# Layer 2 of a mixed FNet/H3 kernel: two sums of the Fourier matrix made by accumulating transfers instead of VectorE

## The chip, the core and the metric

The kernel runs on one core of a Trainium2 chip. A core has TensorE (PE, matrix products, with its weight loads listed apart as PEld), VectorE (DVE), ScalarE (ACT), GpSimd (POOL) and SyncE (SP), which here only issues transfers. Transfers are carried by 16 DMA engines and can be issued from SP, ACT and POOL. The metric is the device time of one execution in microseconds.

## The reference

Four layers follow one another on a stream `x` of 2048 x 576 float32. The first and the third are the FNet mixing, the second and the fourth an H3 block:

```python
def _A_ref(x, Cr, Ci, Wr, Wi):
    a = jnp.einsum("bsd,ed->bse", x, Wr)
    b = jnp.einsum("bsd,ed->bse", x, Wi)
    return jnp.einsum("ts,bse->bte", Cr, a) - jnp.einsum("ts,bse->bte", Ci, b)
...
x = x + _A_ref(_layernorm(x), ...)
x = x + _B_ref(_layernorm(x), ...)   # short conv, times v, long conv by FFT, gate q
x = x + _A_ref(_layernorm(x), ...)
x = x + _B_ref(_layernorm(x), ...)
```

`Cr` and `Ci` are 2048 x 2048 matrices given as inputs. The result is a real part, `Cr a - Ci b`. The change is in the second FNet layer, called layer 2 in the kernel.

## The kernel before, in words

The kernel multiplies with the sequence matrices first and with the hidden matrices afterwards. All products are float32 made of rounded halves: `split` (L90 to L92) rounds a tile to float32r with an ACT copy (L91, the high half) and takes the rest with a DVE subtraction (L92, the low half). A product then is three matmuls: high by high, high by low, low by high, all of them issued through `mm` at L74.

The order in time is: layer 0 (four blocks of 512 output rows) with the convolution branch woven into it; the first block of layer 2, made directly, up to about 803 us; blocks 1, 2 and 3 of layer 2, made by the Strassen scheme in `strassen()`; and at last the hidden products of layer 2 with the gating and the output, from about 1076 us on.

Strassen treats the real and the imaginary matrix and the two halves of the sequence as a 2 x 2 block matrix. A block `tb` has seven products in the order 5, 1, 6, 2, 7, 3, 4 (`ORDER`), each of four steps `kp`, so 28 steps for a block. A step multiplies two column tiles of C (`i` = 0 and 1, together 128 x 1024 words or 512 KB), and each column tile takes 6 matmuls into two PSUM banks, and 2 more for the remaining columns in products 5, 1, 2 and 4. In the text, "block 1, product 7, step 0" is the first step of the product 7 in `tb` = 1, and the three blocks start at about 803.3, 894.0 and 984.6 us.

`load_step` gets the C operand of a step into SBUF, unsplit:

- product 5: the imaginary matrix, first half plus second half. Two loads of 512 KB, one into a `csum` buffer and one into a `cw` buffer, and a DVE addition of 128 x 1024 words (L881). The sum stays in `SUM[kp]`.
- products 1 and 2: one load into `cw`, which is the operand, and a DVE addition of it onto `SUM[kp]` (L891).
- products 6 and 3: `SUM[kp]` as it then stands.
- product 7: the real plus the imaginary matrix, first half. Two loads into two `cw` buffers and a DVE addition (L887).
- product 4: one load into `cw`.

There are four `cw` buffers, three in the region `ph` and one in the region `flts`, and four `csum` buffers, all in `flts`; so a row of the profile that reads `flts,ph` in one of these additions has its `csum` or one `cw` buffer in `flts`. Buffers are used in turn, and the next load into a buffer waits for the last reader of what it held. The loads go out on SP (`load_after`, L161), in one order, and SP waits in order.

`ahead` keeps the load calls four steps and the split calls five column tiles in front of the matmuls. Five `cs` buffers hold the split column tiles, so the split of a column tile can't begin before TensorE has finished with the fifth one before it. Each engine runs its own instructions in order and waits at each for what it reads. In block 3, SP also brings back weights (`mats<-wd`) and results of earlier blocks (`ud`) between these loads.

POOL issues transfers for the convolution branch (L165) and computes powers for the norms (L177, L631). It has neither between the start of block 1 and 1076 us.

Of the kernel before, what the change touches and what calls it, by code (L numbers as in the profile page):

```python
# [13 lines left out]
OP = mybir.AluOpType  # L14
# [4 lines left out]
J = S // P  # L19
# [45 lines left out]
def fnet_h3_kernel(ctx: ExitStack, tc: tile.TileContext, x, c_mat, w_re, w_im, k_pad, v, shift_k,  # L65
                   ssm_k, ssm_d, f1c, i2c, midc, out):
    nc = tc.nc
# [91 lines left out]
    def load_after(dst, src):  # L159
        with tc.issue_after(anchor[-1]):  # L160
            return nc.sync.dma_start(dst, src).ins  # L161
# [689 lines left out]
    def post(tag="post"):  # L851
        return two(ring[tag]())
# [17 lines left out]
    def raw_c(g, tb, s2, kp, tag="cw"):  # L870
        t = post(tag)
        k = 2 * kp + (J // 2 if s2 else 0)
        anchor.append(load_after(t, c_mat[g, tb, k:k + 2].rearrange("k p n -> p k n")))
        return t

    SUM, RAW, HU = {}, {}, {}

    def load_step(tb, m, kp):
        if m == 5:
            src = SUM[kp] = raw_c(1, tb, False, kp, "csum")  # L880
            nc.vector.tensor_tensor(src, src, raw_c(1, tb, True, kp), OP.add)  # L881
        elif m in (6, 3):
            src = SUM[kp]
        elif m == 7:
            r = raw_c(1, tb, False, kp)
            src = raw_c(0, tb, False, kp)
            nc.vector.tensor_tensor(src, src, r, OP.add)  # L887
        else:
            src = raw_c(1 if m == 4 else 0, tb, m != 1, kp)
            if m in (1, 2):  # L890
                nc.vector.tensor_tensor(SUM[kp], SUM[kp], src, OP.add)  # L891
        RAW[tb, m, kp] = src
# [29 lines left out]
    def ahead(loads, halves):  # L922
        while len(RAW) < min(loads, len(steps)):
            load_step(*steps[len(RAW)])
        while len(done) < min(halves, 2 * len(steps)):
            h = len(done)
            done.append(h)
            cs[h] = split_half(steps[h // 2], h % 2)
# [197 lines left out]
```

## Time and profile before

| | us |
|---|---|
| median of 3 runs | 1201.41 |
| lowest, highest | 1200.62, 1201.98 |
| span of the profiled execution | 1198.9 |
| TensorE busy in the span | 1178.8 |
| VectorE busy | 839.6 |
| ScalarE busy | 665.4 |
| GpSimd busy | 74.7 |

The span runs from the first to the last instruction of one execution; the page gives no other time for that execution. The median of the runs lies 2.5 us above the span. The DMA share over the span is 53.9% for the queue of SP, 10.2% for that of ACT and 3.9% for that of POOL. In the profile a busy TensorE is modelled from pipelined matmuls, so its waits are best read from the idle time before an instruction and from the chain of waits.

### The profile page before, as it was taken

What the parts mean: (1) busy time and instruction counts of PE and PEld (TensorE: products, weight loads), DVE (VectorE), ACT (ScalarE), POOL (GpSimd) and SP (SyncE); (2) the same over time, 40 slices, a digit from 0 to 9 for tenths busy, and PEclk for the clock granted to TensorE, in tenths of its full rate; (3) what the DMA queues carried; (4) which work ended last, traced back from release to release, by engine and by line L of the source; (5) the groups of instructions that cost most, each with busy time, mean ns of one, the idle gap of its engine ahead of it and who ended that gap; (6) DMA issues with size and microseconds to landing.
All of it is one profiled execution on the core that took longest, in us unless ns stands there. A gap on an engine that the chain in (4) does not pass through costs nothing.

```text
span 1198.9 us, 18258 instructions
## 1 busy us (share of the span) xinstructions
PE 1178.8 (98%) x6320; PEld 1025.6 (86%) x6320; DVE 839.6 (70%) x1498; ACT 665.4 (55%) x1335; POOL 74.7 (6%) x116
## 2 busy tenths in 40 slices
PE   7999999999999999999999999999999999999997
PEld 6888888988888888888988898888888888789997
DVE  7899983679777677675347766775776777774764
ACT  7855665679877668774435666544444445450210
POOL 2210000000000000001101121000000000001111
PEclk9999999999999999999999999999999999999999
DMA  9869898546766667648967686872682677795621
GB/s 356 292 225 311 282 299 243 188 133 184 219 188 199 213 172 210 193 134 267 291 207 233 221 255 212 272 267 71 216 283 72 208 285 260 238 338 156 218 88 40
DMA packets 146110, 261.95 MB, mean 218 GB/s; under 512 B 15841, under 2 KB 44769, under 8 KB 146018
## 3 DMA queue, kind: packets, MB, share of 16 engines
q1 hardware_dynamic: 102674, 205.58, 53.9%
q10 hardware_dynamic: 36432, 42.63, 10.2%
q0 software_dynamic: 6912, 12.59, 3.9%
q8 instruction: 49, 0.80, 0.3%
q14 instruction: 43, 0.35, 0.1%
HBM read 194.09 MB, written 66.65 MB: 217 GB/s over the span
## 4 chain that ended last, share of the span: by engine, by line
PE 89%; ACT 4%; DVE 3%; DMA 2%; issue 2%; POOL 0%; ACTq 0%; SPq 0%; POOLq 0%; DVEq 0%
PE s L74 50%; PE bk L74 34%; PE rm L74 5%; ACT flts L490 2%; ACT mid L490 1%; DMA flts<-in_c_mat 1%; DVE mats L92 0%; ACT mats L91 0%; ACT u L91 0%; DMA flts<-in_ssm_k 0%; DMA ph<-in_c_mat 0%; DMA wd<-w 0%; DVE u L92 0%; DVE mid L496 0%; DVE f1f L386 0%
## 5 line engine op out<-in xcount | busy, mean ns | idle before, releaser
L74 PE MATMUL s<-mats 128*128 128x512 f32 x2088 | 535.0, 391 | 1.2 <-DVE u L92 0.5
L74 PEld LDWEIGHTS s<-mats 128*128 128x128 f32 x2088 | 380.0, 188 | 70.1 <-DVE u L92 1.1
L92 DVE TENSOR_TENSOR mats<-flts,mats 128x512 fp32r<-128x512 f32 x206 | 140.9, 688 | 63.8 <-ACT mats L91 63.3
L91 ACT ACTIVATE mats<-flts 128x512 fp32r<-128x512 f32 x206 | 128.5, 628 | 84.5 <-PE bk L74 32.3
L74 PEld LDWEIGHTS bk<-mid 128*128 128x128 f32 x768 | 116.2, 188 | 21.7 <-ACT flts L490 8.1
L74 PE MATMUL bk<-mid 128*128 128x288 f32 x768 | 132.5, 299 | 2.2 <-ACT flts L490 2.0
L74 PE MATMUL bk<-w,u 128*128 128x288 f32 x864 | 120.9, 296 | 0.3 <-ACT flts L490 0.3
L74 PEld LDWEIGHTS bk<-w,u 128*128 128x128 f32 x864 | 117.4, 188 | 4.0 <-ACT flts L490 1.9
L496 DVE TENSOR_TENSOR mid<-flts,mid 128x576 fp32r<-128x576 f32 (+1 forms) x149 | 93.5, 628 | 35.2 <-ACT mid L490 32.7
L490 ACT ACTIVATE flts<-bk 128x288 f32<-128x288 f32 x160 | 62.2, 405 | 90.1 <-PE bk L74 81.0
L74 PE MATMUL rm<-mats 128*128 128x512 f32 x304 | 94.9, 391 | 0.0
L490 ACT ACTIVATE flts<-flts 64x288 f32<-64x288 f32 x192 | 85.0, 443 | 5.5
L490 ACT ACTIVATE mid<-flts 128x576 fp32r<-128x576 f32 (+1 forms) x148 | 80.3, 575 | 6.0 <-DMA flts<-t 3.0
L436 ACT ACTIVATE flts<-bk 128x288 f32<-128x288 f32 x128 | 49.3, 410 | 49.9 <-PE bk L74 41.3
L74 PE MATMUL bk<-f1r 128*128 128x288 f32 x384 | 64.2, 300 | 7.7 <-ACT f1r L91 7.6
L74 PEld LDWEIGHTS bk<-f1r 128*128 128x128 f32 x384 | 59.0, 191 | 14.8 <-ACT f1r L91 8.6
L280 DVE TENSOR_TENSOR flts<-flts,bk 128x288 f32<-128x288 f32 x48 | 21.8, 453 | 67.6 <-PE bk L74 67.6
L74 PE MATMUL bk<-mats 128*128 128x288 f32 (+1 forms) x376 | 67.8, 317 | 0.0
L74 PEld LDWEIGHTS rm<-mats 128*128 128x128 f32 x304 | 56.9, 188 | 12.3 <-DVE flts L266 0.3
L74 PE MATMUL s<-t,mats 128*128 128x512 f32 x264 | 64.9, 389 | 0.0
L177 POOL TENSOR_TENSOR flts<-flts 128x1 f32<-128x1 f32 x35 | 29.4, 841 | 522.2 <-DVE flts L176 522.2
L74 PE MATMUL bk<-mats,t 128*128 128x288 f32 (+1 forms) x368 | 59.3, 303 | 0.0
(145 smaller groups left out, 1505.4 us busy)
## 6 DMA issues: line engine op xcount, KB each, us to landing
flts<-in_c_mat SPq DMA_DIRECT2D x148, 256.0 KB, 3.8
ph<-in_c_mat SPq DMA_DIRECT2D x54, 512.0 KB, 4.5
t<-flts ACTq DMA_DIRECT2D x64, 288.0 KB, 4.5
flts<-in_c_mat SPq DMA_DIRECT2D x30, 512.0 KB, 5.3
flts<-t SPq DMA_DIRECT2D x53, 288.0 KB, 2.9
vd<-flts ACTq DMA_DIRECT2D x64, 144.0 KB, 2.3
flts<-vd SPq DMA_DIRECT2D x32, 288.0 KB, 4.5
mid<-in_i2c POOLq DMA_DIRECT2D x32, 256.0 KB, 4.9
```

Source lines behind the costliest of these rows:

```text
L74: nc.tensor.matmul(ps, lhsT, rhs, start=first, stop=last, skip_group_check=more)
L91: a = nc.scalar.activation(h, src, AF.Copy).ins
L92: return a, nc.vector.tensor_tensor(l, src, h.bitcast(F32), OP.subtract).ins
L177: pows.append(nc.gpsimd.tensor_tensor(rs, ve, mhalf, OP.pow).ins)
L280: added[:] = [nc.vector.tensor_tensor(r[:, cs], r[:, cs], ps[:, :HD], OP.add).ins]
L436: stored[:] = [nc.scalar.activation(so[:, c, :], ps[:, :HD], AF.Copy).ins]
L490: last_act.append(nc.scalar.activation(*args, **kw).ins)
L496: nc.vector.tensor_tensor(l, src, h.bitcast(F32), OP.subtract)
```

## The change

In products 5 and 7 of a block, the second of the two matrices is no longer loaded into a buffer of its own and added by VectorE. The first one is loaded by SP as before, into the `csum` buffer (product 5) or a `cw` buffer (product 7), and then a transfer issued from GpSimd reads the second one from memory and adds it onto that buffer (`accum_op=OP.add`). That makes 24 additions and 24 loads from SP fewer, and 24 transfers from GpSimd more. In product 7 the operands change places: the imaginary matrix is loaded, and the real one is added. A `cw` buffer is no longer taken for the second matrix.

```diff
+    def add_c(t, g, tb, s2, kp):
+        k = 2 * kp + (J // 2 if s2 else 0)
+        nc.gpsimd.dma_start(t, c_mat[g, tb, k:k + 2].rearrange("k p n -> p k n"), accum_op=OP.add)
+
     SUM, RAW, HU = {}, {}, {}

     def load_step(tb, m, kp):
         if m == 5:
             src = SUM[kp] = raw_c(1, tb, False, kp, "csum")
-            nc.vector.tensor_tensor(src, src, raw_c(1, tb, True, kp), OP.add)
+            add_c(src, 1, tb, True, kp)
         elif m in (6, 3):
             src = SUM[kp]
         elif m == 7:
-            r = raw_c(1, tb, False, kp)
-            src = raw_c(0, tb, False, kp)
-            nc.vector.tensor_tensor(src, src, r, OP.add)
+            src = raw_c(1, tb, False, kp)
+            add_c(src, 0, tb, False, kp)
         else:
             src = raw_c(1 if m == 4 else 0, tb, m != 1, kp)
```

The order of the matmuls is the same in both kernels, and the other instructions of VectorE and ScalarE keep their order but for a few splits and stores.

## The prediction

> **What bounds the kernel.** I read the page's busy rows first, then the stages of layer 2 as time windows, TensorE's waits, and the chain that ended last.
>
> ```profile
> span 1198.9 us, 18258 instructions
> PE 1178.8 (98%) x6320; PEld 1025.6 (86%) x6320; DVE 839.6 (70%) x1498; ACT 665.4 (55%) x1335; POOL 74.7 (6%) x116
> ```
>
> TensorE is the bound over the whole span. The windows of the Strassen blocks say whether that holds where the edit is:
>
> ```profile
> core 0: us, PE busy (x) PEld busy (x) DVE busy (x) ACT busy (x) POOL busy (x), PEclk, DMA share, GB/s
> 832.30:857.70 25.40, 25.40 (x114) 21.04 (x113) 19.07 (x25) 11.22 (x19) 0.00 (x0) 1.00 0.43 131
> 894.00:984.60 90.60, 90.60 (x400) 74.83 (x399) 62.93 (x84) 39.24 (x64) 0.00 (x0) 1.00 0.59 189
> 1039.00:1050.00 11.00, 10.07 (x45) 8.02 (x44) 6.96 (x10) 5.16 (x10) 0.00 (x0) 1.00 0.88 256
> ```
>
> Block 2 (894.0 to 984.6) has 400 matmuls without a gap, with VectorE at 62.93 of 90.60 us and POOL at nothing. Only the window from 1039 is short of TensorE work, by 0.93 us. TensorE's waits from 803 to 1077 us are one line, and the chain of waits shows what lies behind it:
>
> ```profile
> PE s L74 <- DVE mats L92: 0.9, 1, 0.9
> ```
>
> ```profile
> 1040.01 5.14 DMA flts<-in_c_mat
> ...
> 1045.24 1.23 DVE flts L887
> 1046.47 0.61 DVE mats L92
> ...
> 1047.12 12.99 PE s L74 x56
> ```
>
> This is product 7 of block 3. The last of its additions (L887) stood on VectorE waiting for a transfer until 1045.24; the low half of a column tile that was long in SBUF came behind it, and TensorE waited for that one. So all that VectorE's additions cost the end of the program is 0.9 us.
>
> **What the change removes.** 24 additions:
>
> ```profile
> L881 DVE TENSOR_TENSOR flts<-flts,ph 128x1024 f32<-128x1024 f32 x9 | 11.0, 1222 | 10.5 <-DMA ph<-in_c_mat 10.5
> L887 DVE TENSOR_TENSOR flts<-flts,ph 128x1024 f32<-128x1024 f32 x6 | 7.3, 1225 | 10.0 <-DMA flts<-in_c_mat 9.9
> L887 DVE TENSOR_TENSOR ph<-ph 128x1024 f32<-128x1024 f32 x6 | 7.3, 1220 | 1.3 <-DMA ph<-in_c_mat 1.3
> L881 DVE TENSOR_TENSOR flts<-flts 128x1024 f32<-128x1024 f32 x3 | 3.7, 1225 | 1.9 <-DMA flts<-in_c_mat 1.9
> ```
>
> That is 11.0 + 7.3 + 7.3 + 3.7 = 29.3 us of VectorE, and 23.7 us in which it stood waiting for a transfer ahead of them. All of it but the 0.9 us lies beside TensorE's work, so removing it is worth 0.9 us: -0.9. SP loses 24 issues that it makes between waits: nothing.
>
> **What it adds.** 24 accumulating transfers on POOL. Issuing them is hidden: POOL is idle in these windows. What counts is latency. Before, the two loads ran side by side, and a 1.2 us addition followed. Now the second transfer can't be issued before the first has landed, and the splits wait for both one after the other. No accumulating transfer is in the trace, so its time from issue to landing, X, is bounded by the nearest rows:
>
> ```profile
> flts<-in_c_mat SPq DMA_DIRECT2D x148, 256.0 KB, 3.8
> ph<-in_c_mat SPq DMA_DIRECT2D x54, 512.0 KB, 4.5
> flts<-in_c_mat SPq DMA_DIRECT2D x30, 512.0 KB, 5.3
> mid<-in_i2c POOLq DMA_DIRECT2D x32, 256.0 KB, 4.9
> ud<-ph ACTq DMA_DIRECT2D x12, 512.0 KB, 5.8
> ph<-in_c_mat SPq DMA_DIRECT2D x12, 256.0 KB, 3.5
> ```
>
> ```profile
> L165 POOL DMA_DIRECT2D mid<-in_i2c x32: 527/527/535, 363.9 to 602.4; - x32
> DMA to landing us min/median/max: 2.9/5.1/7.3
> ```
>
> ```profile
> L161 SPq DMA_DIRECT2D ph<-in_c_mat x66: 327/368/622, 747.9 to 1047.6; - x66
> DMA to landing us min/median/max: 2.1/3.9/7.8
> ```
>
> The second fence is line 165 (POOL's loads of 256 KB), the third line 161 (SP's). From below, X is 2.9 us, the fastest load that POOL issued. From above I take two full transfers in a row, as slow as the slowest of POOL and of SP: 7.3 + 7.8 = 15.1 us. Between them: a POOL load takes 4.9 us for 256 KB; going to 512 KB costs SP 1.0 (`ph`, 3.5 to 4.5) to 1.5 us (`flts`, 3.8 to 5.3), so 6.2 for 512 KB; and an accumulation must also read the buffer out, for which the nearest row is the 512 KB store at 5.8 us. If reading in and reading out don't overlap, X = 6.2 + 5.8 = 12.0 us. I take that value: an addition needs both operands before it can write, and no row shows these overlapping. A POOL issue of 256 KB takes 0.53 us, so 24 of double size are at most 24 x 1.06 = 25 us of an idle engine.
>
> **Where X meets TensorE: product 7.** Its load needs a `cw` buffer, and that comes free with the low-half split of the product 2 step that held it. These are the last such splits of steps 0 to 3, in block 1 and in block 3 (VectorE's timeline):
>
> ```profile
> 839.81 0.69 DVE L92 TENSOR_TENSOR mats<-ph,mats 128x512 fp32r<-128x512 f32 x1 [0.17 <-ACT mats L91]
> 842.53 0.69 DVE L92 TENSOR_TENSOR t<-ph,t 128x512 fp32r<-128x512 f32 x1 [0.67 <-ACT t L91]
> 846.19 0.68 DVE L92 TENSOR_TENSOR mats<-ph,mats 128x512 fp32r<-128x512 f32 x1
> 849.10 0.69 DVE L92 TENSOR_TENSOR mats<-flts,mats 128x512 fp32r<-128x512 f32 x1 [0.49 <-ACT mats L91]
> ```
>
> ```profile
> 1021.63 0.68 DVE L92 TENSOR_TENSOR t<-ph,t 128x512 fp32r<-128x512 f32 x1
> 1024.00 0.69 DVE L92 TENSOR_TENSOR mats<-ph,mats 128x512 fp32r<-128x512 f32 x1 [0.29 <-ACT mats L91]
> 1027.66 0.68 DVE L92 TENSOR_TENSOR mats<-ph,mats 128x512 fp32r<-128x512 f32 x1
> 1031.97 0.68 DVE L92 TENSOR_TENSOR t<-flts,t 128x512 fp32r<-128x512 f32 x1
> ```
>
> And this is when TensorE begins product 7 in these blocks (chain; timeline). Its 12 matmuls a step run 2.72 us (6 take 1.36):
>
> ```profile
> 855.88 1.36 PE s L74 x6
> ...
> 857.69 23.13 PE s L74 x102
> ```
>
> ```profile
> 1039.00 4.24 PE L74 MATMUL s<-mats,t 128*128 128x512 f32 x18
> ```
>
> A split is 0.69 us on VectorE (rows above) after 0.63 on ScalarE, so a sum must have landed 1.3 us before its step:
>
> ```profile
> L91 ACT ACTIVATE mats<-ph 128x512 fp32r<-128x512 f32 x47 | 29.6, 629 | 33.5 <-PE bk L74 15.8 <-PE s L74 8.3 <-DVE mats L92 4.4
> ```
>
> Block 1: buffers free at 840.5, 843.2, 846.9, 849.8; loads landed (4.5, 4.5, 4.5, and 5.3 us for the one in `flts`) at 845.0, 847.7, 851.4, 855.1; sums needed at 856.4, 859.1, 861.8, 864.5. That leaves X 11.4, 11.4, 10.4 and 9.4 us. Block 2 has the same spacing. Block 3: free at 1022.3, 1024.7, 1028.3, 1032.7; landed at 1026.8, 1029.2, 1032.8, 1038.0; needed at 1037.7, 1040.4, 1043.1, 1045.9; X may take 10.9, 11.2, 10.3 and 7.9 us. The last step is the tightest everywhere. With X = 12.0 TensorE waits 2.6 us in blocks 1 and 2 and 4.1 in block 3: +9.3 in sum. A wait at an earlier step is part of it, since it moves all later needs.
>
> Behind the waiting split on ScalarE stand the copies that empty product 2's banks, on VectorE the remainder sum. Their banks are needed by product 3, 10.9 us after product 7 begins, so they add nothing.
>
> **Product 5** has more room. Its first load of block 1 goes out at 781.28 and block 1 begins at 803.29:
>
> ```profile
> 781.28 0.43 SPq L161 DMA_DIRECT2D flts<-in_c_mat  x1
> ```
>
> ```profile
> 803.29 1.36 PE s L74 x6
> ```
>
> 781.3 + 5.3 + 12.0 = 798.6, and it is needed at 802.0; the waits begin at X over 15.4. Later blocks load when product 3's splits free the buffer, near 868.6, and need the sum by 894: over 20 us for 17.3. Nothing.
>
> **Sum.** +9.3 - 0.9 = +8.4 us. The profiled execution spans 1198.9 us, 2.5 below the median of the runs; I take that offset as unchanged: 1201.4 + 8.4 = 1209.8 us. The runs of before lie within 0.11%, so about 0.2% (2.4 us) is what can be told from no change. By the bounds of X: at 15.1 the waits are 5.7 + 5.7 + 7.2 - 0.9 = +17.7, so 1219.1; at 9.4 and less only block 3 waits, by at most 1.5.
>
> **The rivals.**
> Hidden transfer (not slower): if X stays below 7.9 us, every sum lands in time, the 0.9 us goes, and the time is 1200.5. For it: DMA share is only 0.43 in the window in which block 1's accumulations would run, and the loads start a buffer round earlier than before, since product 7 takes 4 buffers and not 8. It decides at X = 9.4 (blocks 1 and 2). The Trainium skill speaks for it: "DMA: Bandwidth & Descriptors", section on the anatomy of a gpsimd DMA, gives 2.0 us plus bytes over 436 GB/s, and "Collectives: The Full Stack", section on the bandwidth ceiling, says that a reducing transfer costs two source reads and not the adding. By them an estimate of X is 2.0 + 2 x 1.2 = 4.4 us and the time 1200.5. Against the first page, the trace has 4.9 us for a POOL load of 256 KB, where that rule gives 2.6; whether the reads overlap no trace here shows.
>
> Slow adding: if the DMA engines add at a third or less of their copying rate, X is 15 to 25 us. At 20 us the waits are 10.6 + 10.6 + 12.1, and product 5 of block 1 adds 4.6, less 0.9: 1238. Nothing in the profile speaks for or against a rate of adding.
>
> Accumulations one at a time: if each starts only when the one before has landed, step 3 of product 7 lands at 845.0 + 4 x 12.0 = 893.0 where 864.5 is needed: 28.5 us a block, 1201.4 + 85 = 1287. POOL's loads before were issued far apart, so the rows don't exclude it.
>
> **How the numbers follow.** Forecast (X from 10.0 to 15.1): 0.42, with its own range 1203.8 to 1219.1. Hidden, within 0.2%: 0.31. Slow adding: 0.15. One at a time: 0.08. Faster by over 0.2%: 0.04, for which no wait of that size is in the blocks. Slower is 0.42 + 0.15 + 0.08 = 0.65. The range from 1200.0 to 1235.0 holds the forecast, the hidden case and about half of the slow adding, 0.81.
>
> **What would show it.** The landing time of the POOL transfers of line 878: near 12 us, or below 9.4. TensorE's waits in product 7, on a split (L91 or L92) that waits for the accumulation: 2 to 4 us in each block, most in block 3. No wait on VectorE for a C load at 1040 to 1045. Loads of product 7 issued at about 840.5, 843, 847 and 850. The forecast is wrong if X is short (reads overlap), or if product 5's sums are late.

## The result, and the profile after

The changed kernel takes 1211.99 us in the median of 4 runs (1210.13 to 1214.23), against 1201.16 us for the kernel before. The ratio is 1.0094, with a 95% interval of 1.0079 to 1.0110: slower by 0.9%. The profiled execution took 1213.06 us, of which 1211.0 are the span, 12.1 us more than the span before.

The page of the changed kernel: span, busy rows, and the queue of POOL (packets, MB, share of the 16 DMA engines).

```profile
span 1211.0 us, 18268 instructions
PE 1185.3 (98%) x6320; PEld 1027.4 (85%) x6320; DVE 813.2 (67%) x1474; ACT 665.0 (55%) x1335; POOL 103.4 (9%) x140
q0 software_dynamic: 13440, 25.17, 9.7%
```

VectorE does 26.4 us less, and the program is longer. TensorE's waits in the Strassen blocks (803 to 1090 us; total, count, longest) were 0.9 us in all and are now 6.5 us:

```profile
PE s L74 <- ACT mats L91: 2.7, 3, 1.6
PE s L74 <- ACT t L91: 2.3, 1, 2.3
PE s L74 <- DVE mats L92: 1.1, 4, 0.3
PE s L74 <- DVE t L92: 0.4, 2, 0.2
```

The accumulating transfers are line 878 of the changed kernel. Its source view shows POOL's time for an issue (ns, minimum, median, maximum) and the time from issue to landing:

```profile
L878 POOL DMA_DIRECT2D flts<-in_c_mat x15: 1179/1189/1251, 786.6 to 1049.1; - x15
L878 POOL DMA_DIRECT2D ph<-in_c_mat x9: 1179/1189/1196, 845.5 to 1045.1; - x9
...
DMA to landing us min/median/max: 5.6/9.0/15.9
```

The chain of block 1, product 7, step 3 (start, duration, what):

```profile
850.86 7.13 DMA flts<-in_c_mat
...
858.03 0.50 issue
858.53 9.89 DMA flts<-in_c_mat
...
868.53 0.64 ACT t L91
...
869.19 0.70 DVE t L92
...
869.94 10.27 PE s L74 x37
```

The load lands after 7.13 us, POOL needs 0.54 us until it has issued, the accumulation takes 9.89 us; then come the two splits, and TensorE, which stood until 869.94. TensorE's timeline at that place, and at the same place of block 2:

```profile
869.21 0.50 PE L74 MATMUL s<-t 128*128 128x512 f32 x1 [2.32 <-ACT t L91]
869.94 2.42 PE L74 MATMUL s<-t 128*128 128x512 f32 x5 [0.23 <-DVE t L92]
```

```profile
963.91 0.50 PE L74 MATMUL s<-mats,t 128*128 128x512 f32 x1 [1.65 <-ACT mats L91]
```

The 5 matmuls from 869.94 take 2.42 us. Elsewhere 6 take 1.36. Windows of the changed kernel show the reason (PE, PEld, DVE, ACT and POOL busy, then the granted clock, the DMA share and GB/s):

```profile
870.00:871.50 1.50, 1.50 (x4) 1.21 (x5) 1.50 (x3) 1.26 (x3) 0.00 (x0) 0.52 0.24 55
871.50:873.00 1.50, 1.50 (x5) 1.12 (x4) 0.79 (x2) 0.60 (x1) 0.00 (x0) 0.50 0.42 158
873.00:874.50 1.50, 1.50 (x7) 1.22 (x6) 1.43 (x3) 0.17 (x2) 0.00 (x0) 0.84 1.03 395
...
966.00:969.00 3.00, 3.00 (x8) 2.32 (x7) 2.41 (x5) 0.75 (x2) 0.00 (x0) 0.50 0.70 257
```

After each of these two waits the clock is granted at half for 3.41 us, which costs 1.7 us of matmul time. Before had no such stretch in the Strassen blocks. And block 3 has a wait in front of the last columns that was not there (chain of the changed kernel):

```profile
1065.75 8.37 DMA mats<-ud
...
1074.14 0.63 ACT mats L91
...
1076.06 0.69 DVE mats L92
...
1076.80 1.43 PE s L74 x5
```

All 6320 matmuls stand in both traces in the same order, so the loss can be read off the difference of their start times. It is worked out from both traces, matmul by matmul:

| place | later than before by, us | of that |
|---|---|---|
| before block 1 | 1.0 | the instructions there are the same; the other kernels below stand here between -0.8 and +1.0 |
| block 1 | 4.7 | wait in product 7: 3.0; half clock: 1.7 |
| block 2 | 3.9 | wait in product 7: 2.3; half clock: 1.6 |
| block 3 | 3.3 | waits in product 7: 2.2; the old wait gone: -1.2; later waits: 2.1; rest 0.2 |

The three blocks lose 11.9 us. The waits read this way are longer than the 6.5 us of the view of waits. One reason stands in the rows above: the matmul alone at 869.21 is listed as busy for 0.50 us, while in a row of six each takes 0.23 (1.36 / 6).

### The profile page after: what moved, and what is told of

It reads as the page before. It is cut to its first block, busy times and chain, and to the rows that moved or that the text cites. A ratio compares the mean times of both kernels' runs of the same rounds, so it can differ in the third digit from the quotient of the medians.

```text
span 1211.0 us, 18268 instructions
## 1 busy us (share of the span) xinstructions
PE 1185.3 (98%) x6320; PEld 1027.4 (85%) x6320; DVE 813.2 (67%) x1474; ACT 665.0 (55%) x1335; POOL 103.4 (9%) x140
## 4 chain that ended last, share of the span: by engine, by line
PE 84%; DMA 7%; ACT 4%; DVE 3%; issue 2%; POOL 0%; SPq 0%; ACTq 0%; POOLq 0%; DVEq 0%
PE s L74 46%; PE bk L74 33%; PE rm L74 5%; DMA flts<-in_c_mat 5%; ACT flts L490 2%; ACT mid L490 1%; DMA t<-flts 1%; DMA mats<-ud 1%; ACT mats L91 1%; DVE mats L92 1%; DMA early<-in_x 0%; ACT u L91 0%; DVE u L92 0%; DVE f1f L386 0%; DVE f1f L391 0%
## 5 line engine op out<-in xcount | busy, mean ns | idle before, releaser
L92 DVE TENSOR_TENSOR mats<-flts,mats 128x512 fp32r<-128x512 f32 x201 | 137.5, 688 | 83.8 <-ACT mats L91 83.3
L91 ACT ACTIVATE mats<-flts 128x512 fp32r<-128x512 f32 x201 | 125.4, 628 | 78.6 <-PE bk L74 31.4
L92 DVE TENSOR_TENSOR mats<-ph,mats 128x512 fp32r<-128x512 f32 x52 | 35.6, 688 | 37.9 <-ACT mats L91 37.9
L91 ACT ACTIVATE mats<-ph 128x512 fp32r<-128x512 f32 x52 | 32.4, 629 | 50.3 <-DMA ph<-in_c_mat 16.6
```

What stands on the lines that cost most here:

```text
L91: a = nc.scalar.activation(h, src, AF.Copy).ins
L92: return a, nc.vector.tensor_tensor(l, src, h.bitcast(F32), OP.subtract).ins
```

## The experiments

My first theory was that of the prediction: in product 7 a load and an accumulation come one after the other, the lead time of step 3 is too short for the pair, and product 5 costs nothing. Its rivals were that the adding transfers load the DMA engines and slow whatever runs beside them, and that the loss comes from another part of the change. Losses by block are differences of start times against before, as in the table.

**One product at a time.** First product 5 alone (product 7 as before), then product 7 alone.

```diff
         elif m == 7:
-            src = raw_c(1, tb, False, kp)
-            add_c(src, 0, tb, False, kp)
+            r = raw_c(1, tb, False, kp)
+            src = raw_c(0, tb, False, kp)
+            nc.vector.tensor_tensor(src, src, r, OP.add)
```

> Only product 5 accumulates; product 7 is as before (two loads from SP and a VectorE addition). Theory A (the loss is product 7's chain of load and accumulation, product 5's sums land long before they are needed): the time of before, 1200 to 1202 us, ratio 0.999 to 1.001, no wait of TensorE in product 5. Theory B (accumulating transfers burden the DMA engines, so each of the 24 costs its share, 10.8 / 24 = 0.45 us): half of the loss, about 1206.5 us.

Measured: 1201.85 us, ratio 1.0008 (1.0000 to 1.0017). The blocks lose 0.16 us in all; TensorE's only wait is the old one:

```profile
PE s L74 <- DVE mats L92: 1.2, 1, 1.2
```

```diff
         if m == 5:
             src = SUM[kp] = raw_c(1, tb, False, kp, "csum")
-            add_c(src, 1, tb, True, kp)
+            nc.vector.tensor_tensor(src, src, raw_c(1, tb, True, kp), OP.add)
```

> Only product 7 accumulates; product 5 is as before. Theory A: the whole loss, 1210 to 1214 us, ratio near 1.009, with the waits of TensorE at step 2 or 3 of product 7 and two stretches at a granted clock of 0.50. Theory B: half of the loss, about 1206.5 us.

Measured: 1213.02 us, ratio 1.0110 (1.0094 to 1.0125). Losses of 5.0, 0.9 and 4.0 us, with two stretches of half clock. Its chain in block 1 has the same two transfers:

```profile
850.52 7.39 DMA flts<-in_c_mat
...
858.48 10.23 DMA flts<-in_c_mat
```

So the whole loss is product 7's, and product 5 is free, as forecast. Which block loses how much differs between the two kernels. In block 2 the wait is 0.9 us here and brings no half clock; in the changed kernel it is 2.3 us, and the half clock adds 1.6.

**The adding taken away.** The same transfers in the same order without `accum_op`; the second matrix overwrites the first, so the first is left out of the sum.

```diff
-        nc.gpsimd.dma_start(t, c_mat[...], accum_op=OP.add)
+        nc.gpsimd.dma_start(t, c_mat[...])
```

> All 24 POOL transfers stay, with their waits and bytes from memory, but they overwrite the buffer and don't add (the first matrix is left out of both sums). Theory A with the accumulation itself as the slow part: a plain POOL transfer of 512 KB lands in 5 to 7 us where the accumulating one took 9.9, step 3's data lands near 864 and the time is 1200 to 1203 us. If the two transfers in a row are enough by themselves, whatever they do: 1208 us or more.

Measured: 1202.5 us, ratio 1.0017 (1.0008 to 1.0026). Line 878 in this kernel:

```profile
L878 POOL DMA_DIRECT2D flts<-in_c_mat x15: 722/722/752, 786.2 to 1038.0; - x15
...
DMA to landing us min/median/max: 4.7/6.3/8.5
```

Blocks 1 and 2 are on time (-0.0 and -0.1 us) although the second transfer still follows the first, so the order of the two alone is not enough to make TensorE wait. At the median of all 24 transfers the adding costs 9.0 - 6.3 = 2.7 us of landing time, but that median mixes both products and all steps. At step 3 of product 7, which decides, the plain transfers land after 4.79, 5.17 and 4.87 us in blocks 1, 2 and 3, the accumulating ones after 9.89, 8.99 and 8.51: the adding costs 3.6 to 5.1 us there. The load in front of it is shorter too, 5.19, 4.37 and 5.98 us against 7.13, 7.34 and 7.58. These are block 1's load and plain transfer (views of transfers from 849.5 to 852 and from 855.7 to 856.5 us):

```profile
flts<-in_c_mat SPq DMA_DIRECT2D x1, 512.0 KB, 5.2
...
flts<-in_c_mat POOLq DMA_DIRECT2D x1, 512.0 KB, 4.8
```

So without the adding the whole chain of block 1 is 5.19 + 0.55 + 4.79 = 10.5 us, where the changed kernel has 17.6. The time on the DMA engines is in the rows of POOL's queue, before and in this kernel:

```profile
q0 software_dynamic: 6912, 12.59, 3.9%
...
q0 software_dynamic: 10368, 25.17, 7.0%
```

The first 12.59 MB are the convolution branch's in every kernel. The 24 transfers of C therefore take 7.0 - 3.9 = 3.1% of the engines plain, and 9.7 - 3.9 = 5.8% with the adding, 1.9 times as much for the same bytes from memory.

In block 3 the old wait is gone, worth 1.2 us, and 1.3 us come back some 15 us later, in front of a column tile that waits for a result of an earlier block (chain of this kernel, and its waits from 803 us on):

```profile
1054.12 7.96 DMA mats<-ud
```

```profile
PE s L74 <- ACT mats L91: 0.4, 1, 0.4
PE s L74 <- DVE mats L92: 0.3, 1, 0.3
```

This bears on a term of the prediction: the 0.9 us that VectorE's wait cost is no gain to be had here by itself, as TensorE meets the next late transfer.

**The accumulation twice.** In product 7 the accumulation is issued twice, so the real matrix counts twice; product 5 is as before.

```diff
             src = raw_c(1, tb, False, kp)
             add_c(src, 0, tb, False, kp)
+            add_c(src, 0, tb, False, kp)
```

> Product 5 as before; in product 7 the real matrix is accumulated twice, one transfer after the other (its output lacks the right sum: the real matrix counts twice). Theory A (chain length): step 3's sum lands one landing time later, 8 to 10 us and 0.5 us of waiting to issue, and TensorE waits that much longer in each block: about 1211 + 3 x 9.5 = 1240 us, 1235 to 1246. Theory B (a price for each transfer on the DMA engines): as much again as the 12 accumulations of product 7 cost, 1222 us.

Measured: 1243.11 us (one run), 30.1 us above product 7 alone. The blocks lose 14.5, 14.7 and 14.7 us. A second accumulation thus costs some 10 us a block on the mean (30.1 / 3). Part of that is the clock: the Strassen blocks have seven stretches at half of it, where product 7 alone has two. TensorE's waits by the view are 29.9 us against 6.6, which is 7.8 more a block. Step 3's second accumulation lands 8.24, 8.56 and 9.62 us after its issue; a chain with no slack left would give waits of about that size.

**The accumulation in two halves.** Each accumulation as two transfers of 256 KB, one a column tile, so that the first tile needn't wait for the second.

```diff
-        nc.gpsimd.dma_start(t, c_mat[...], accum_op=OP.add)
+        for i in range(2):
+            nc.gpsimd.dma_start(t[:, i, :], c_mat[g, tb, k + i], accum_op=OP.add)
```

> Each accumulation is issued as two of 256 KB, one for each column tile. Theory A with a landing time that grows with the bytes: the first column tile lands 2 to 4 us sooner, and the second is needed 1.36 us later than the first, so the waits of a block fall from about 3 us to 0 to 1 us and the clock stays at 1.00: 1201 to 1205 us. If an accumulating transfer has a mostly fixed price and queues behind the one before: the second half lands later than the whole did, 1212 us or more.

Measured: 1208.6 us, ratio 1.0065 (1.0052 to 1.0077), above what was expected. The halves don't land in half the time. In block 1, step 3, the load takes 7.27 us and the second half 9.03 (chain):

```profile
849.93 7.27 DMA flts<-in_c_mat
...
858.29 9.03 DMA flts<-in_c_mat
```

The blocks lose 1.6, 2.7 and 4.3 us. The waits come in pieces of at most 0.6 us and the clock stays up:

```profile
862.00:870.00 8.00, 7.50 (x30) 5.20 (x29) 3.32 (x6) 3.86 (x7) 0.00 (x0) 1.00 0.85 241
870.00:873.00 3.00, 3.00 (x15) 2.48 (x14) 2.96 (x5) 0.89 (x3) 0.00 (x0) 1.00 0.95 272
```

**Load and accumulation in halves.** The missing half of the last experiment: in product 7 the load too is split by column tile, so that the first accumulation begins when the first 256 KB have landed. Bytes, buffers and product 5 are as in the changed kernel.

```diff
         elif m == 7:
-            src = raw_c(1, tb, False, kp)
-            add_c(src, 0, tb, False, kp)
+            src = post("cw")
+            for i in range(2):
+                anchor.append(load_after(src[:, i, :], c_mat[1, tb, 2 * kp + i]))
+            for i in range(2):
+                nc.gpsimd.dma_start(src[:, i, :], c_mat[0, tb, 2 * kp + i], accum_op=OP.add)
```

> As the changed kernel, but in product 7 the load of the first matrix and the accumulation both go in two transfers of 256 KB, one for each column tile, so that a column tile's accumulation waits for its own half alone and starts when its half of the buffer is free. Theory A (lead time of product 7's chain is all that is missing): against the kernel that halved the accumulations only, each column tile gets 2 us or more of lead, where that one lost 1.5 us in block 1, so the waits of blocks 1 and 2 go and the time is 1201 to 1204 us, with the clock at 1.00. If the bytes of the accumulation are what is short (DMA engines full at 850 to 865 us), the time stays with that kernel, near 1208.6 us.

Measured: 1203.21 us, ratio 1.0018 (1.0009 to 1.0027). Blocks 1 and 2 lose nothing (0.0 and -0.1 us); TensorE has no wait there. ScalarE's timeline (first fence) shows the first tile of step 3 split at 861.01; in the changed kernel it was 868.53. A window of this kernel (second) and the same one of the changed kernel (third) show the DMA engines as loaded in the one as in the other, a share of 1.07 and 1.02:

```profile
861.01 0.63 ACT L91 ACTIVATE t<-flts 128x512 fp32r<-128x512 f32 x1 [0.63 <-DMA flts<-in_c_mat]
```

```profile
850.00:868.00 18.00, 18.00 (x81) 14.92 (x80) 8.12 (x12) 9.15 (x15) 3.42 (x4) 1.00 1.07 285
```

```profile
850.00:868.00 18.00, 16.89 (x75) 13.66 (x73) 5.35 (x8) 5.25 (x10) 2.38 (x2) 1.00 1.02 250
```

The queue of POOL has the same 9.7%. With the same bytes and the same load on the engines TensorE doesn't wait in blocks 1 and 2, so it is the time from the load's issue to the sum that decides, and not the traffic as such. Traffic counts as far as it lengthens this chain, as the load in front of step 3 shows (7.13 us, and 5.19 without the adding). Block 3 still loses 2.4 us, in waits of 0.2 to 0.4.

**Accumulating only where the lead is long.** Steps 0 and 1 of product 7 accumulate; steps 2 and 3 load both matrices and add on VectorE.

```diff
+            r = raw_c(1, tb, False, kp) if kp > 1 else None
+            src = raw_c(0 if kp > 1 else 1, tb, False, kp)
+            if kp > 1:
+                nc.vector.tensor_tensor(src, src, r, OP.add)
+            else:
+                add_c(src, 0, tb, False, kp)
```

> Product 5 as before; in product 7 only steps 0 and 1 accumulate, steps 2 and 3 load twice and add on VectorE. Theory A says that the last steps are the tight ones (slack 11.4 us at steps 0 and 1, 9.4 at step 3): the clock stays at 1.00 and the time is 1200 to 1204 us. If steps 0 and 1 already miss their column tiles: 1206 us or more.

Measured: 1209.14 us, ratio 1.0079 (1.0063 to 1.0096), above what was expected. The edit does more than was meant. Steps 2 and 3 now take four `cw` buffers, and two of these are held by the accumulations of steps 0 and 1. The chain of block 1 ends on a VectorE addition in the way of a split:

```profile
863.90 1.23 DVE ph L892
865.13 0.61 DVE t L92
```

So the run says nothing of the lead of steps 0 and 1 alone. It does speak on the clock: waits of 1.5 and 1.8 us in blocks 1 and 2 brought no half clock, one of 1.9 in block 3 did (the last section shows why).

**Another way to the 0.9 us.** Since all that there was to gain was VectorE's wait in block 3, the addition can stay on VectorE and stand behind the low-half split that it held up. No transfer accumulates; `low` lists the low-half splits, and `R7` keeps the matrix that was loaded first until it is added.

```diff
     def split_half(step, i):
+        tb, m, kp = step
+        if m == 7 and i == 0:
+            with tc.issue_after(low[-1]):
+                nc.vector.tensor_tensor(RAW[step], RAW[step], R7[tb, kp], OP.add)
         c = two(ring["cs"]())
-        split(c[:, 0], c[:, 1], RAW[step][:, i, :])
+        low.append(split(c[:, 0], c[:, 1], RAW[step][:, i, :])[1])
```

> No accumulation anywhere: the kernel before, with each VectorE addition of product 7 placed behind the low-half split of the column tile ahead of it. If TensorE's only wait of the Strassen blocks comes from the addition standing in front of that split, the wait of 0.9 us in block 3 goes: 1200 us, ratio 0.999 to 1.000. If the last sum is late itself, or another wait takes its place (as in the kernel without adding, where 1.2 us were won at product 7 and 1.3 lost behind it): no change, 1201 us.

Measured: 1202.15 us, ratio 1.0011 (1.0002 to 1.0020). The old wait is gone, and a result that comes back from an earlier block stands in front of step 3's tile instead (chain and TensorE's timeline):

```profile
1042.65 6.35 DMA t<-ud
```

```profile
1050.75 0.50 PE L74 MATMUL s<-mats,t 128*128 128x512 f32 x1 [1.31 <-ACT mats L91]
```

The clock is at half for 3.41 us behind that wait, and this profiled execution is the longest of the eleven, 1204.08 us.

The same with product 5 accumulating:

> The same placing of product 7's additions, and product 5 accumulates by GpSimd. If product 5's accumulations are free, the same time as with the placing alone, 1199.5 to 1201 us, and no wait of TensorE in product 7; if they delay other loads, 1202 us or more.

Measured: 1202.15 us, ratio 1.0014 (1.0005 to 1.0023), with waits of 0.8 and 0.6 us and the clock up in these blocks. Then `split_u`, which splits that result, put behind the last split of C as well, without and with the accumulating product 5:

```diff
-            if sg > 0:
-                split_in(h, l)
+            with tc.issue_after(low[-1]):
+                if sg > 0:
+                    split_in(h, l)
```

> No accumulation: the kernel with product 7's additions placed late, and the splits of the reloaded results (u_d) placed behind the column tiles of C that were called before. If the wait that took the place of the first one came from those splits, standing in front of a column tile while they wait for their load, TensorE has no wait of over 0.3 us in the Strassen blocks and the Strassen part is 1.0 us shorter than before: 1199.5 to 1200.5 us, ratio 0.999. If a third wait follows: 1201 or more.

Measured: 1202.72 us, ratio 1.0014 (1.0005 to 1.0023). TensorE still waits, now for the last sum itself:

```profile
PE s L74 <- ACT mats L91: 1.5, 1, 1.5
...
```

> The same placing, and product 5 accumulates by GpSimd. Product 5's accumulations are free: same as the kernel with the placing alone, 1199.5 to 1200.5 us. If they slow other loads: 1201 us or more.

Measured: 1203.18 us, ratio 1.0020 (1.0010 to 1.0029), with waits of 0.6 and 0.5 us. No version beats the kernel before. In block 3 the DMA engines are full; the kernel before has a share of 1.00 in this window, and in the kept traces each reordering changed which transfer or which sum came last:

```profile
1052.00:1068.00 16.00, 16.00 (x72) 13.25 (x71) 14.04 (x24) 11.39 (x21) 0.00 (x0) 1.00 1.00 358
```

## Why the prediction was right, and where it was off

It forecast 1209.8 us and slower; measured were 1211.99. The mechanism held, and several terms were off in ways that partly cancelled.

- *Product 5 free*: right. Alone it costs 0.16 us in the blocks.
- *Loads of product 7 at 840.5, 843, 847 and 850*: right; the last went out at 850.86 in a trace that is 1.0 us late at that place.
- *X = 12.0 us*: too long. The median is 9.0, step 3's 9.89 in block 1 and 8.99 in block 2. I took reading in and reading out as one after the other (6.2 + 5.8). At step 3 the plain transfer takes 4.8 to 5.2 us and the adding puts 3.6 to 5.1 on it, so both parts were taken too long. That the two follow one another is not shown: these times don't tell it from a reading in and a reading out that overlap and share the engines.
- *Load in front of it, 5.3 us*: too short. It took 7.13 to 7.58 us. It now runs beside accumulations of the earlier steps, with the DMA share at 1.02. With plain transfers in their place the same load took 5.19, 4.37 and 5.98 us, about what was forecast, so it is their adding that lengthens it. The prediction let the adding act on its own transfer alone.
- *What lies between them*: I priced nothing. The chain has 0.54 us from the landing of the load to the issue of the accumulation.
- These three together, 7.13 + 0.54 + 9.89 = 17.56 us in block 1, stand against 17.3 forecast. That is why the waits of product 7 in blocks 1 and 2 (3.0 and 2.3 us) are near the forecast 2.6 each: the sum was right by two errors of opposite sign, which is luck.
- *Most in block 3, 4.1 us*: wrong. Its waits in product 7 are 2.2 us, though the chain is nearly as long as in block 1: 7.58 + 0.57 + 8.51 = 16.66 us. The step that failed is the time at which the buffer comes free, 1032.7, which I carried over from before. In the changed kernel (first fence, chain of block 3) the split that frees it ends at 1040.90. Blocks 1 and 2 and the start had made the trace 9.6 us late by then, so it is 1042.3 - 1040.9 = 1.4 us earlier than it would have been. What had held it up stands in VectorE's timeline of before (second fence): an addition of product 7, which waited 1.28 us for its load and ran 1.22.

```profile
1040.20 0.70 DVE t L92
...
1040.92 7.58 DMA flts<-in_c_mat
...
1049.07 8.51 DMA flts<-in_c_mat
```

```profile
1029.62 1.22 DVE L887 TENSOR_TENSOR ph<-ph 128x1024 f32<-128x1024 f32 x1 [1.28 <-DMA ph<-in_c_mat]
```

With that the room for load and accumulation in block 3 is 5.3 + 7.9 + 1.4 = 14.6 us, and 16.66 - 14.6 = 2.1 us of wait, against 2.2 in the table. The same sum gives 17.56 - 14.7 = 2.9 in block 1. That the addition and its wait were the cause is shown by the kernel with late additions, where this one stands behind the split and nothing accumulates: its split ends at 1032.00 in a trace that is 0.7 us late there, also 1.4 us earlier than before. With product 5 alone accumulating, the addition stays but no longer waits, and the split ends 1.1 us earlier.

- *-0.9 for VectorE's wait*: the old wait went, and was worth 1.2 us at its place; but later waits in block 3 cost 2.1 us. Plain transfers give it back too (1.3), so this part is not due to the adding.
- *The half clock*, 3.3 us in all, was in no term. With the waits of product 7 (7.5), the old wait (-1.2) and the later ones (2.1) it makes 11.7 of the 11.9 us.
- *POOL's issues*, put at 25 us or less in all: they took 28.7 us (24 of about 1.19). POOL has no other work there, so the time doesn't hang on it.
- *The rivals*: the hidden transfer needed X under 7.9 us; 9.0 is above, though plain transfers would have been hidden. The fastest accumulation, 5.6 us, would have been too. A rate of adding of a third is out: the DMA engines' time for the same bytes grows 1.9 times (3.1% to 5.8% of the span), and product 7's accumulations land within 10 us there, not 15 to 25. One at a time is out as well: step 3's sum landed at 868.4, and not near 893.

## What to carry to other kernels

Moving an addition from a compute engine into an accumulating transfer turns two parallel loads into a chain, so count the lead time from the moment the buffer comes free to the first use, with a load under the new contention, the issuing engine's reaction and the slower landing, before counting the instructions saved; and count too which buffers come free earlier on the engine that is relieved. An addition that is hidden beside TensorE is worth nothing, and the one wait that it causes is worth only the distance to the next late transfer. Where such a chain is a little too long, starting it in smaller pieces (load and accumulation both) can recover most of it with the same bytes moved. Compare landing times at the step that is tight: a median over all transfers showed 2.7 us for the adding where the tight step paid 3.6 to 5.1.

## What was unexpected in the hardware

- An accumulating transfer of 512 KB into SBUF lands 9.0 us after its issue at the median (5.6 to 15.9) and takes 1.19 us of POOL to issue; the same transfer without adding takes 6.3 us (4.7 to 8.5) and 0.72 us. How much the adding costs depends on what runs beside it: the first accumulation of each block's product 7 lands after 5.8, 5.6 and 7.1 us (plain 5.2, 4.7 and 5.2), while the four of product 5 before block 1, issued within 4.4 us, take 9.9, 12.4, 14.8 and 15.9 (plain 6.6 to 8.5). By a rule of the Trainium skill, "DMA: Bandwidth & Descriptors", section on the anatomy of a gpsimd DMA, an estimate is 2.0 us plus bytes over 436 GB/s, 3.2 us for one read of 512 KB and 4.4 for two; both measurements are well above.
- A wait of TensorE of 2.3 or 1.65 us, each followed by 0.23, brought 3.41 us at half the clock, and so did 1.31 with 0.38, and one of 1.9. Waits of 1.5 with 0.3, and of 1.8, in other kernels did not, and none of 0.6 or less did. So length alone doesn't decide in this range; where the wait lies does. In the clock records of a trace the changes fall on a fixed beat: in the changed kernel the half clock begins at 870.05 and 965.63 us, 28 x 3.413 apart, and with the accumulation twice at 861.10, 871.34, 966.91, 977.15, 1072.72, 1082.96 and 1089.79, all whole multiples of 3.413 apart. Cut by this beat, these are the windows of the two longer waits of the kernel that accumulates in steps 0 and 1:

```profile
957.26:960.68 3.42, 2.12 (x9) 1.76 (x10) 3.26 (x6) 2.69 (x5) 0.00 (x0) 1.00 0.15 15
1049.42:1052.84 3.42, 1.53 (x7) 1.17 (x7) 3.12 (x5) 1.96 (x4) 0.00 (x0) 1.00 0.40 141
```

  The wait of 1.8 us lies across the start of the first window, which keeps 2.12 us of matmuls, and the clock stays; the one of 1.9 lies whole in the second, which has 1.53, and the clock is at half in the next. In the kept traces each window of the Strassen blocks with 1.72 us of matmuls or less was followed by half the clock, but for one with 1.72, and none with 1.88 or more was; half a window is 1.71. The Trainium skill, "TensorE: Matmul & The Clock Gate", Part 1, says that the clock falls after an idle window of about 3.4 us and comes back after a busy one, and that the window runs freely. The length of 3.41 us and the fixed beat agree with that; but a window about half idle is enough here, and none had to be idle throughout.
